# Gate and up stage: the first logit sum of four blocks moved behind the up-weights' sums and parts on VectorE

## The chip, the core and the metric

The kernel runs on one core of one Trainium2 chip. The metric is the device time of one execution in microseconds (us); lower is better.

## What is computed

A token's output is a gated mix of a Fourier layer and a GEGLU layer, with S = 2048 tokens, D = 640, F = 1728, all float32:

```python
g = _sigmoid((x * gate_w).sum(-1, keepdims=True))
a = jnp.einsum("bsd,ed->bse", x, dft_hid_re)
b = jnp.einsum("bsd,ed->bse", x, dft_hid_im)
y = jnp.einsum("ts,bse->bte", dft_seq_re, a) - jnp.einsum("ts,bse->bte", dft_seq_im, b)
b = (_gelu(x @ w_gate) * (x @ w_up)) @ w_down
return g * y + (1 - g) * b
```

The argument of the sigmoid, one number per token, is the *logit* of the title.

## The kernel before

Every matrix product is made of three products of float32r parts (`mm3`, L99 to L103): an operand is split into a high part (ScalarE, `high`, L82) and a low part (VectorE, `low`, L85, what the high part left out), and high x high, low x high and high x low are summed in a bank of 128x512. To save products, blocks of two rows and two columns are multiplied by Strassen's scheme, so VectorE also forms sums and differences of weights, of inputs and of results.

The kernel has four stages: a first block, the gate and up stage (blocks f = 1 to 12 of the 1728 hidden columns), the product with w_down, and the Fourier layer. The change lies in the gate and up stage. Its loop (L1179) issues each block's products from generators (`gate_up`, `together`, `together_up`), and between them takes small pieces of other work from a queue, `fills` (L1153 to L1163): a piece is a cost and a function, and pieces are taken in order, as many as the products issued so far allow. Inside the stage, TensorE, ScalarE, VectorE and POOL keep the order in which the code is written (`in_order`, L107). So the order of `fills` is VectorE's order.

Blocks 5, 7, 9 and 11 are the first of a pair of blocks that share products. In them `fills` holds, ahead of the next block's weights:

- four pieces left over from the block before (`last_sums`, `last_sum`, L578 to L586): differences of results, stored to `hT` by POOL (L404);
- the up-weights across the pair (`make_up`, L241): `across` forms four sums of 128x128 in the raw tile `wu5r` (L246 to L249), `high_u` makes `wu5h` on ScalarE, `low_u` makes `wu5l` (L85); the digit in these names is the block;
- `sum_wd` (L606): sums of down-weights in `dr` and `da` (L595 to L600), stored to `wsd` by SP (L602);
- two logit sums (`load_z`, L709): each loads a tile `xz` of 128x640 (SP, L716) and multiplies it by the gate weights, with a sum along the row (VectorE, L720, followed by a read-back of the accumulator, also L720). The first tile is loaded ahead of the queue, the second where the first sum is done.

Other names in the rows: `pH5t`, `pZ5t` and `pH5u`, `pZ5u` are banks of the shared products, for gate and up; L454 adds `pH5t` to a result that frees the bank, as the copies by ScalarE at L148 do; `xq` and `xu` are shared inputs, loaded anew by POOL in each such block (`load_across`, L1150), three `xu` tiles in each; `hA` and `hT` are stores of results by POOL; L309 forms a difference in the raw weights of the next block, which ScalarE then splits.

Tiles of 4 KB a partition, `xz` among them, share a pool of 46 buffers (`slot`, L72). A tile gets a buffer that an earlier tile gave back, in the order in which the code asks, and the first writer of the new tile waits for the last reader of the old one.

Of the kernel before, what the change touches and what calls it, by code (L numbers as in the profile page):

```python
# [37 lines left out]
def kernel(  # L38
# [68 lines left out]
    @contextmanager  # L107
    def in_order(*engines):

        traced = nc.cur_bb.bb.instructions  # L110
        mark = traced[-1]
        yield
        start = next(k for k in reversed(range(len(traced))) if traced[k] is mark) + 1
        dep = mybir.DependencyInfo(mybir.DependencyClass.NoSync, mybir.DependencyReason.DATA)
        prev = {}
        for ins in traced[start:]:
            if ins.engine in engines:
                if ins.engine in prev:
                    tc.add_manual_dep(ins, prev[ins.engine].name, dep, reason="in_order")
                prev[ins.engine] = ins  # L120
# [84 lines left out]
    def pair_of(f):  # L205


        return 0 if f < PAIRED or f >= NF else 2 - (f - PAIRED + 1) % 2
# [18 lines left out]
    def load_up(f):  # L227

        r = slot(F32, [P, 8, P], f"wu{f}r")
        nc.sync.dma_start(r[:, 0:2], wf[f, :, 2:4])  # L230
        nc.sync.dma_start(r[:, 6:8], wf[f - 1, :, 2:4])
        return r
# [8 lines left out]
    def make_up(f, r):  # L241

        W, own = {}, {}

        def across():
            tt(r[:, 2], r[:, 0], r[:, 1], op=ALU.add)  # L246
            tt(r[:, 4], r[:, 6], r[:, 0], op=ALU.subtract)
            tt(r[:, 3], r[:, 2], r[:, 6], op=ALU.subtract)
            tt(r[:, 5], r[:, 7], r[:, 3], op=ALU.subtract)  # L249

        def high_u():
            own["u"] = [slot(F32R, [P, 8, P], f"wu{f}{n}") for n in "hl"]
            high(own["u"][0][:, 1:6], r[:, 1:6])

        def low_u():
            u = own["u"]
            low(u[0][:, 1:6], u[1][:, 1:6], r[:, 1:6])
            W["A22p"] = at(u, 1)
            for k in range(4):
                W[f"S{k + 1}p"] = at(u, 2 + k)  # L260

        return W, [(112, across), (0, high_u), (78, low_u)]
# [343 lines left out]
    def sum_wd(k):  # L606

        work = []

        def load():  # L610
            r, a21 = slot(F32, [P, 8, P], f"dr{k}"), wsmall(F32, f"da{k}")
            nc.sync.dma_start(r, wd[k, :, :8])
            nc.sync.dma_start(a21, wd[k, :, 8:])
            work.extend(do for _, do in sums_left(nc.sync, r[:, 0:2], r[:, 2:4], r[:, 6:8], a21, wsd[k]))

        def do():
            work.pop(0)()

        return [(0, load), (84, do), (84, do)]
# [89 lines left out]
    def load_z(n):  # L709

        r, work = {}, []

        def load():
            sb = zq.pop(0)
            r[0] = sb, slot(F32, [P, D], f"xz{sb}")
            nc.sync.dma_start(r[0][1], xz[sb])  # L716

        def total():
            sb, v = r.pop(0)
            nc.vector.tensor_tensor_reduce(v, v, gwb, 1.0, 0.0, ALU.mult, ALU.add, z[:, sb : sb + 1])  # L720

        return [(0, load), (80, total)] * n
# [66 lines left out]
    def load_k(i):  # L789


        tp, b, k = kseq[i]
        n = f"{tp}{b}{k}"
        r = None
        if not (k == NK and b):
            r = slot(F32, [P, 8, P], f"kw{n}")
        if k == NK and b:
            src = hL[tp]
        elif k == NK:
            m = slot(F32, [P, 8, P], f"km{n}")  # L800
            d = slot(F32, [P, 8, P], f"kd{n}")
            nc.sync.dma_start(r[:, :5], wd0)
            for q in range(2):
                rows = slice(q * FR, (q + 1) * FR)
                nc.sync.dma_start(m[rows, :5], wdr)
                nc.sync.dma_start(d[rows, :4], wd0[:FR, :4])
            r, src = (r, m, d), h0[tp]
        elif b:
            nc.sync.dma_start(r[:, 0:2], wd[k, :, 6:8])
            nc.sync.dma_start(r[:, 2:8], wsd[k][:, 0:6])  # L810
            src = hT[tp][k]
        else:
            nc.sync.dma_start(r[:, 0:6], wd[k, :, 0:6])
            nc.sync.dma_start(r[:, 6:8], wsd[k][:, 6:8])
            src = hA[tp][k]
        raw = []
        for q in range(2):
            raw.append(pair(F32, f"kr{n}{q}"))
            nc.sync.dma_start(raw[q], src[:, 2 * q : 2 * q + 2])
        kraw[i] = r, raw  # L820
# [332 lines left out]
    fills, state = deque(), {}  # L1153
# [24 lines left out]
    with in_order(PE, ACT, DVE, POOL):  # L1178
        for f in range(1, NF):  # L1179
            kind = pair_of(f)  # L1180
            if f == PAIRED:
                loadu()
                fills.extend([*t4, *u123[:3], *late_work, *u123[3:], *u4])
            fills.extend(todo)
            todo.clear()
            if kind == 1:
                up, work = make_up(f, load_up(f))
                fills.extend(work)
            if kind == 1:
                lw, *w = sum_wd((f - PAIRED) // 2)  # L1190
                lw[1]()
                fills.extend(w)
            if f == PAIRED - 1:
                loadp()
                fills.extend(t123)
            if f == NF - 1:
                lw, *w = sum_wd(NK - 1)
                lw[1]()
                fills.extend(w)
            if f + 1 < NF:  # L1200
                nxt, work = make_w(f + 1)
                if kind != 1 or f == PAIRED:
                    fills.extend(work)
            if kind == 1 and f > PAIRED:
                (_, first), z1, (_, second), z2 = load_z(2)
                first()
                k = len(fills) // 2
                more = list(fills)
                fills.clear()
                fills.extend([*more[:k], z1, (0, second), *more[k:], z2, *work])  # L1210
            elif f in ZE_AT:
                (_, first), z1 = load_z(1)
                first()
                fills.insert(5, z1)
            if f == NF - 1:
                load_k(0)
                fills.extend(split_pieces(0))
                gates(0)
                nc.scalar.activation(table, table, AF.Gelu_apprx_tanh)
            state.update(pe=0, done=0, all=sum(c for c, _ in fills), pe_all=2450 if not kind else 2994 if kind == 1 else 1768)  # L1220
            s5 = pair(F32, f"s5{f}")
            xs = {}
            work = [gate_up(f, W, Bs[tp], tp, s5[:, tp], s1t, xs, s4) for tp in range(2)]
            more = together(f, W, Tp, s1t, xs) if kind == 1 else iter(())
            more_up = together_up(f, W, up, s4) if kind == 1 else iter(())
            store_left()
            if f in LEFT_AT:
                left_work.extend(LEFT_AT[f]())
                if f in (2, 12):
                    k = len(fills) // (2 if f == 2 else 1)  # L1230
                    rest = [fills.pop() for _ in range(len(fills) - k)]
                    fills.extend([*left_work, *reversed(rest)])
                    state["all"] = sum(c for c, _ in fills)
                    left_work.clear()
            for _ in range(4):
                run(more)
            for step in range(8 if not kind else 7):
                for tp, w in enumerate(work):
                    run(w)
                    if (step, tp) in ((0, 1), (1, 1)):  # L1240
                        run(more)
                        if step == 0:
                            run(more)
                    if (2, 0) < (step, tp) < (6, 0):
                        run(more_up)
                if step < 2 and kind == 1 and f > PAIRED:
                    for k in ((1,), (2, 3))[step]:
                        load_across(f, "xu", Tu, keptu, k)
                if step == 4 and pair_of(f + 1) == 1 and f + 1 > PAIRED:
                    for k in (1, 2, 3):  # L1250
                        load_across(f + 1, "xq", Tp, keptp, k)
                if step == 5:
                    load_w(f + 2)
                if f == NF - 1 and step > 4:
                    load_k(step - 4)
            for v in (more, more_up):
                next(v, None)
            while fills:
                fills.popleft()[1]()
            W = nxt  # L1260
# [438 lines left out]
```

## Time and profile before

| what | value |
|---|---|
| median of 3 runs | 1020.55 us (1020.52 to 1021.36) |
| the profiled execution, its own time | 1021.83 us |
| its span, first to last instruction | 1020.0 us |
| TensorE busy (PE), weight loads (PEld) | 1015.6 us, 840.2 us |
| VectorE busy (DVE) | 823.2 us |
| ScalarE busy (ACT) | 486.1 us |
| GpSimd busy (POOL) | 166.9 us |
| granted TensorE clock | 1.00 |

How to read it: busy time is the time in which an engine executes; weight loads run beside the products before. Rows of a timeline give the start, the duration, the engine, the source line, the operation and "out<-in", and in brackets how long the engine sat idle before it and what ended that. "SPq" is a row of a queue that only issues DMAs. An `x2` counts merged rows. Times in the text are from the start of the span. Blocks 5, 7, 9 and 11 lie at about 145, 193, 241 and 289 us.

### The profile page before, as it was taken

Reading aid. Unit: us, or ns where it says so; the run is one execution under the profiler, and the core shown is the slowest. Engines: PE = TensorE matmul, PEld = TensorE weight load, DVE = VectorE, ACT = ScalarE, POOL = GpSimd, SP = SyncE. Lnnn points to the kernel's source line nnn. Section 1 sums busy time; section 2 is a strip of 40 time slices with the busy share of each in tenths; the row PEclk is TensorE's granted clock in tenths of the full one; section 3 lists DMA queues with packets and bytes.
Section 4 is the critical chain, followed back from the end, with each engine's and each line's share of the span. In section 5 each row is a group of like instructions: output and inputs, shape, how many; then the busy total and the mean of one; then the engine's idle time right before and its main releaser. Section 6 shows DMA issues by size and latency. Waiting matters only on the chain.

```text
span 1020.0 us, 13269 instructions
## 1 busy us (share of the span) xinstructions
PE 1015.6 (100%) x4483; PEld 840.2 (82%) x4483; DVE 823.2 (81%) x1154; ACT 486.1 (48%) x622; POOL 166.9 (16%) x295
## 2 busy tenths in 40 slices
PE   9999999999999999999999999999999999999998
PEld 7888888888888888888888888888888888888887
DVE  6987877787787989888887976898588869797796
ACT  5544534353535667557444443444344444455440
POOL 0122242323231200100001012102210200021112
PEclk9999999999999999999999999999999999999999
DMA  7468588968699999979874669668866877897856
GB/s 271 168 209 276 181 264 275 314 225 290 201 315 313 415 374 383 330 245 329 295 254 172 213 223 337 223 200 298 302 203 209 294 252 275 295 349 215 274 134 99
DMA packets 96644, 267.58 MB, mean 262 GB/s; under 512 B 12672, under 2 KB 27008, under 8 KB 96576
## 3 DMA queue, kind: packets, MB, share of 16 engines
q1 hardware_dynamic: 70512, 185.24, 53.2%
q0 software_dynamic: 25776, 81.30, 24.4%
q8 instruction: 35, 0.57, 0.2%
q14 instruction: 33, 0.27, 0.1%
q10 hardware_dynamic: 288, 0.20, 0.1%
HBM read 192.48 MB, written 70.27 MB: 258 GB/s over the span
## 4 chain that ended last, share of the span: by engine, by line
PE 97%; issue 1%; DMA 1%; DVE 0%; POOL 0%; POOLq 0%
PE pX L103 6%; PE pX L102 6%; PE pX L101 6%; PE pZ L103 4%; PE pZ L102 4%; PE pZ L101 4%; PE pL L102 3%; PE pL L103 3%; PE pL L101 3%; PE pV L102 2%; PE pV L103 2%; PE pV L101 2%; PE pY L102 1%; PE pR L103 1%; PE pQ L101 1%; PE pQ L102 1%
## 5 line engine op out<-in xcount | busy, mean ns | idle before, releaser
L82 ACT ACTIVATE ch<-csa 128x1024 fp32r<-128x1024 f32 x32 | 34.0, 1063 | 78.2 <-DVE csa L770 76.7
L85 DVE TENSOR_TENSOR cl<-cra,ch 128x1024 fp32r<-128x1024 f32 x32 | 39.1, 1222 | 24.6 <-ACT ch L82 22.5
L82 ACT ACTIVATE ch<-cra 128x1024 fp32r<-128x1024 f32 x32 | 33.9, 1059 | 52.3 <-DVE cl L85 19.3
L85 DVE TENSOR_TENSOR cl<-crb,ch 128x1024 fp32r<-128x1024 f32 x32 | 39.1, 1223 | 14.4 <-ACT ch L82 14.4
L102 PE MATMUL pL<-cl,xah 128*128 128x512 f32 x128 | 49.9, 390 | 0.0
L103 PE MATMUL pL<-ch,xal 128*128 128x512 f32 x128 | 49.9, 390 | 0.0
L101 PE MATMUL pL<-ch,xah 128*128 128x512 f32 x128 | 49.7, 390 | 0.0
L82 ACT ACTIVATE ch<-crb 128x1024 fp32r<-128x1024 f32 x32 | 33.8, 1055 | 31.2 <-PE pL L102 11.4
L404 POOL DMA_DIRECT2D hA<-s x48 | 26.1, 544 | 132.7 <-DVE s L562 113.1
L85 DVE TENSOR_TENSOR cl<-csb,ch 128x1024 fp32r<-128x1024 f32 x32 | 39.2, 1225 | 3.7 <-ACT ch L82 2.3
L85 DVE TENSOR_TENSOR cl<-csa,ch 128x1024 fp32r<-128x1024 f32 x32 | 39.1, 1221 | 2.1 <-ACT ch L82 1.1
L82 ACT ACTIVATE ch<-csb 128x1024 fp32r<-128x1024 f32 x32 | 34.0, 1062 | 11.7 <-DVE csb L773 4.7
L556 ACT ACTIVATE s<-s 128x512 f32<-128x512 f32 x24 | 15.2, 633 | 46.7 <-DVE s L555 46.7
L148 ACT ACTIVATE s<-pX 128x512 f32<-128x512 f32 x40 | 23.5, 598 | 23.7 <-PE pX L103 22.4
L85 DVE TENSOR_TENSOR kl<-kw,kh 128x1024 fp32r<-128x1024 f32 x24 | 29.4, 1223 | 4.5 <-DMA kw<-in_wd 2.6
L82 ACT ACTIVATE kh<-kw 128x1024 fp32r<-128x1024 f32 x24 | 25.3, 1052 | 16.1 <-PE kR L103 6.2
L551 DVE TENSOR_TENSOR s<-s,pX 128x512 f32<-128x512 f32 x24 | 16.5, 686 | 19.6 <-PE pX L103 14.3
L1346 POOL DMA_DIRECT2D uA<-c x8 | 4.3, 542 | 168.9 <-DVE c L1448 168.7
L404 POOL DMA_DIRECT2D hT<-s x48 | 26.0, 541 | 24.3 <-DVE s L579 8.1
L929 POOL DMA_DIRECT2D out<-ks x12 | 6.5, 541 | 136.8 <-DVE ks L928 136.2
L101 PEld LDWEIGHTS pL<-ch,xah 128*128 128x128 f32 x128 | 24.0, 188 | 5.0
L102 PEld LDWEIGHTS pL<-cl,xah 128*128 128x128 f32 x128 | 24.0, 188 | 5.0
(3612 smaller groups left out, 3483.8 us busy)
## 6 DMA issues: line engine op xcount, KB each, us to landing
cra<-in_ct SPq DMA_DIRECT2D x64, 512.0 KB, 4.6
crb<-in_ct SPq DMA_DIRECT2D x64, 512.0 KB, 5.0
hA<-s POOLq DMA_DIRECT2D x48, 256.0 KB, 5.9
hT<-s POOLq DMA_DIRECT2D x48, 256.0 KB, 5.7
kr<-hA SPq DMA_DIRECT2D x24, 512.0 KB, 7.7
kr<-hT SPq DMA_DIRECT2D x24, 512.0 KB, 6.8
ux<-uA SPq DMA_DIRECT2D x24, 512.0 KB, 5.9
ux<-uT SPq DMA_DIRECT2D x16, 512.0 KB, 6.7
```

The lines of the kernel that those rows point to most:

```text
L82: nc.scalar.activation(hi, raw, AF.Copy)
L85: nc.vector.tensor_tensor(lo, raw, hi.bitcast(F32), op=ALU.subtract)
L101: nc.tensor.matmul(ps, lh, rh, start=first, stop=False, skip_group_check=True)
L102: nc.tensor.matmul(ps, lh, rl, start=False, stop=False, skip_group_check=True)
L103: nc.tensor.matmul(ps, ll, rh, start=False, stop=last, skip_group_check=True)
L148: nc.scalar.activation(m, src, AF.Copy)
L404: nc.gpsimd.dma_start(to[:, i], src)
L551: tt(s5, s5, X, op=ALU.add)
L556: nc.scalar.activation(s2, s2, AF.Gelu_apprx_tanh)
L929: nc.gpsimd.dma_start(acc4[:, t] if tp and e == 4 else out[2 * tp + t, e], src)
L1346: nc.gpsimd.dma_start(to[:, i], src)
```

## The change

One number changes, the place in the queue at which the first sum `z1` and the second load are put:

```diff
             if kind == 1 and f > PAIRED:
                 (_, first), z1, (_, second), z2 = load_z(2)
                 first()
-                k = len(fills) // 2
+                k = len(fills) - 2
                 more = list(fills)
                 fills.clear()
                 fills.extend([*more[:k], z1, (0, second), *more[k:], z2, *work])
```

`fills` has nine pieces there (four left over, three of the up-weights, two of the down-weights), so k goes from 4 to 7: the first sum and the second load stood behind the left-over pieces, and now stand behind the up-weights.

VectorE in block 5 (`xz` and `z` are the logit sum; the number behind a name tells tiles apart):

```order
-L720 ISA xz_1411,z<-xz_1411,gwb 128x640
-L720 ISA z 128x1
-L454 TENSOR_TENSOR s_1431<-s_1431,pH5t 128x512
 L246 TENSOR_TENSOR wu5r<-wu5r 128x128
 L247 TENSOR_TENSOR wu5r<-wu5r 128x128
 L248 TENSOR_TENSOR wu5r<-wu5r 128x128
 L249 TENSOR_TENSOR wu5r<-wu5r 128x128
+L454 TENSOR_TENSOR s_1431<-s_1431,pH5t 128x512
 L459 TENSOR_TENSOR s_1450<-s_1450,pZ5t 128x512
 L460 TENSOR_TENSOR s_1450<-s_1450,pX_1_1461 128x512
 L85 TENSOR_TENSOR wu5l<-wu5r,wu5h 128x640
+L720 ISA xz_1411,z<-xz_1411,gwb 128x640
+L720 ISA z 128x1
 L595 TENSOR_TENSOR dr_1407<-da_1408,dr_1407 128x256
```

The first sum goes from ahead of the up-weights' sums to behind `wu5l`; L454 goes behind the four small sums. Blocks 7, 9 and 11 read the same.

SP in block 5, with the semaphores that each issue waits for (DMAHW and DMASW tell of landed transfers, the others of engines):

```order
 L612 DMA dr1_1407<-in_wd 128x1024 [waits DMASW4_49,DMAHW3_49,DMASW1_49,PE_49]
 L716 DMA xz0_1411<-in_xz 128x640 [waits DMASW4_49,DMASW6_49,DVE_49,DMAHW4_49,PE_49,Activation_49]
-L716 DMA xz1_1482<-in_xz 128x640 [waits DMASW7_49,DMASW5_49,DMAHW5_49,PE_49,Activation_49]
+L716 DMA xz1_1513<-in_xz 128x640 [waits DMAHW2_49,DMAHW5_49,DMAHW1_49,DVE_49]
 L602 DMA wsd1_128<-dr1_1407 128x256 [waits DMAHW6_49,DMAHW3_49,DVE_49]
 L602 DMA wsd1_128<-da1_1408 128x256 [waits DMAHW7_49,DVE_49]
 L602 DMA wsd1_128<-dr1_1407 128x256 [waits DMAHW0_49,DVE_49]
```

The second `xz` load keeps its place in SP's order but has another buffer: it waited for a product on TensorE, and now it waits for VectorE, for L85 `wu5l`, the last reader of `wu5r`, whose buffer it takes. In blocks 7 and 9 it is the same; in block 11 the buffer is one that stores of `hT` read.

POOL in block 5:

```order
 L404 DMA hT11_84<-s53_985 128x512 [waits DMASW1_49,DVE_49]
 L404 DMA hT11_84<-s54_1257 128x512 [waits DMASW2_49,DVE_49]
-L1150 DMA xu51_1490<-xv1_562 128x1024 [waits DMASW3_49,PE_49]
-L1150 DMA xu52_1532<-xv2_563 128x1024 [waits DMAHW1_49,DMAHW2_49,DMASW4_49,DVE_49]
+L1150 DMA xu51_1487<-xv1_562 128x1024 [waits DMASW3_49,PE_49]
+L1150 DMA xu52_1532<-xv2_563 128x1024 [waits DMASW4_49,DVE_49]
 L1150 DMA xu53_1534<-xv3_564 128x1024 [waits DMASW5_49,PE_49]
```

The order is kept, but the second `xu` load (`xu52`) had the buffer of `wu5r` and waited for L85 `wu5l`; now it has the buffer of the first `xz` tile and waits for the first logit sum. Blocks 7 and 9 read the same; in block 11 it waits for a store of `hT`, before and now.

## The prediction, made before the changed kernel ran

> **What bounds the kernel now.** I read the page first, then the waits of TensorE's weight loads in the stretch that holds the four blocks, then the timelines of one of them, engine by engine.
>
> ```profile
> PE 1015.6 (100%) x4483; PEld 840.2 (82%) x4483; DVE 823.2 (81%) x1154; ACT 486.1 (48%) x622; POOL 166.9 (16%) x295
> ```
>
> TensorE is busy for 1015.6 of 1020.0 us, so 4.4 us are idle in the whole span. The list of waits for 150 to 320 us (who waited, for whom, us in total, times, longest) shows what of this lies in the stage:
>
> ```profile
> PEld pH7u L101 <- DMA xu<-xv: 0.5, 1, 0.5
> PEld pH7t L101 <- DVE s L454: 0.2, 1, 0.2
> ```
>
> Two waits, both in block 7. What the first costs shows in the matmul starts (start, duration, engine, line):
>
> ```profile
> 212.27 0.39 PE L102 MATMUL pX<-xT03l,ws7h 128*128 128x512 f32 x1
> 212.50 0.39 PE L103 MATMUL pX<-xT03h,ws7l 128*128 128x512 f32 x1
> 213.01 0.50 PE L101 MATMUL pH7u<-xu,wu7h 128*128 128x512 f32 x1
> 213.34 0.40 PE L102 MATMUL pH7u<-xu,wu7h 128*128 128x512 f32 x1
> ```
>
> Matmuls start 0.23 apart; here 0.51 and 0.33, so 0.28 + 0.10 = 0.38 us are lost. The stage can therefore **give at most 0.38 + 0.2 = 0.6 us** to any reordering, less than 0.2% of the time (2.04 us), about what a measurement of this kernel can tell from no change. What is left to ask is whether the change makes TensorE wait, and for how long.
>
> **The change part by part.** No instruction is added or taken away; four times, one sum of 128x640 moves on VectorE, and one load moves in time. Block 5 on VectorE:
>
> ```profile
> 150.19 0.69 DVE L585 TENSOR_TENSOR s<-s,s 128x512 f32<-128x512 f32 x1
> 153.50 0.83 DVE L720 CUSTOM_DVE_ANT_0 xz<-xz,gwb 128x640 f32<-128x640 f32 x1 [2.62 <-DMA hA<-s]
> 154.25 0.08 DVE L720 DVE_READ_ACCUMULATOR2_ANT z<- 128x1 f32 x1
> 154.25 0.68 DVE L454 TENSOR_TENSOR s<-s,pH5t 128x512 f32<-128x512 f32 x1
> 154.85 0.28 DVE L246 TENSOR_TENSOR wu5r<-wu5r 128x128 f32<-128x128 f32 x1
> ...
> 155.78 0.68 DVE L459 TENSOR_TENSOR s<-s,pZ5t 128x512 f32<-128x512 f32 x1
> ...
> 158.22 0.82 DVE L85 TENSOR_TENSOR wu5l<-wu5r,wu5h 128x640 fp32r<-128x640 f32 x1 [1.04 <-DMA hT<-s]
> 158.97 0.42 DVE L595 TENSOR_TENSOR dr<-da,dr 128x256 f32<-128x256 f32 x1
> ```
>
> *What gets earlier.* The first sum stalls VectorE for 2.62 us at its old place. Without it the four sums of L246 to L249 follow L585 directly (0.60 behind 150.19, as L246 is 0.60 behind L454) and take 0.93 (154.85 to 155.78), so L454 starts at 150.19 + 0.60 + 0.93 = 151.7 instead of 154.25. That is 2.5 us of margin, but only block 7 waits for L454: a gain of 0 to 0.2 us. I take nothing, since a weight load runs ahead of its matmul. The rest of the gain ends at L85 wu5l: it waited 1.04 us for a store of hT, and still does.
>
> *What gets later: the second xu load.* In the changed program it takes the buffer of the first sum's tile, so it waits for that sum, where it waited for L85 wu5l:
>
> ```profile
> 159.45 1.13 POOL L1150 DMA_DIRECT2D xu<-xv  x2 [4.31 <-DVE dr L595]
> xu<-xv POOLq DMA_DIRECT2D x1, 512.0 KB, 5.2
> 164.78 0.19 PEld L101 LDWEIGHTS pH5u<-xu,wu5h 128*128 128x128 f32 x1
> ```
>
> Now L85 wu5l ends at 158.22 + 0.82 = 159.04, and the issue follows 0.41 later. Then the sum starts at 158.97 (where L595 stands) and its read-back ends 0.75 + 0.08 later, at 159.80: **0.76 us later**. The load (the second row is the DMA view of 159.3 to 159.7: KB, us to landing) lands at 159.45 + 5.2 = 164.65 now, and the weight load that needs it starts at 164.78: 0.13 spare. So block 5 would lose 0.76 - 0.13 = 0.63 us, and block 7, whose weight load waits already, all 0.76. In block 9:
>
> ```profile
> L1150 POOL DMA_DIRECT2D xu<-xv x2: 537/544/551, 254.5 to 255.1; - x2
> L101 PEld LDWEIGHTS pH9u<-xu,wu9h x1: 188/188/188, 260.6 to 260.6; 128*128 128x128 f32 x1
> ```
>
> With 5.2 to land it is there at 259.7, 0.9 early, which covers 0.76: nothing. In block 11 the load takes the buffer of a tile that a store of hT reads, not that of the sum; issued at 302.0 and needed at 308.3, it has 1.1 spare, and I count nothing there either:
>
> ```profile
> L1150 POOL DMA_DIRECT2D xu<-xv x2: 540/544/548, 302.0 to 302.6; - x2
> L101 PEld LDWEIGHTS pH11u<-xu,wu11h x1: 188/188/188, 308.3 to 308.3; 128*128 128x128 f32 x1
> ```
>
> The Trainium skill's page "DMA: Bandwidth & Descriptors", section "Anatomy of one DMA — SWDGE (gpsimd) path", fits a load that POOL issues as 2.0 us plus its bytes over 436 GB/s, which for 512 KB gives an estimate of 3.2 us; by that the load would be there 2 us before its use and this whole term would be 0. The row says 5.2, with other transfers around it, and the measurement decides.
>
> *What takes some of it back: the second xz load leaves a crowded place.* The pair of loads in block 5 (first and last start, then us to landing):
>
> ```profile
> L716 SPq DMA_DIRECT2D xz<-in_xz x2: 327/328/328, 144.8 to 147.5; - x2
> ...
> DMA to landing us min/median/max: 7.8/8.2/8.5
> ```
>
> The second was issued at 147.5, in the burst at a block's start, and needed 7.8 us; now it goes into the buffer of wu5r and waits for L85 wu5l, the last reader. First the engines' windows (the last columns are the clock, the DMA share and GB/s), then the two queues from 151.8 to 154.3 us:
>
> ```profile
> 148.00:152.00 4.00, 4.00 (x19) 3.31 (x18) 2.88 (x5) 0.04 (x1) 1.73 (x4) 1.00 1.00 396
> 152.00:156.00 4.00, 4.00 (x19) 3.33 (x18) 2.47 (x8) 0.05 (x1) 1.63 (x3) 1.00 1.04 419
> 160.00:164.00 4.00, 4.00 (x19) 3.27 (x18) 3.72 (x10) 3.97 (x9) 0.54 (x2) 1.00 0.84 206
> ...
> q0 software_dynamic: 225, 0.73, 71.8%
> q1 hardware_dynamic: 144, 0.31, 31.6%
> ```
>
> From 148 to 156 the DMA engines are full (share 1.00 and 1.04), and the 0.31 MB on the hardware queue are about the size of one xz tile (320 KB). At 419 GB/s it takes 0.78 us of them, so the stores of hT behind it, and with them L85 wu5l, come 0 to 0.78 us earlier. The middle is nearest to what the rows say: the store waits for room until 152.4 (POOL's row "152.44 0.54 ... <-DMA hA<-s" stands before most of that traffic), and only its own way from there gains. I take 0.4. In the other direction, the late load now lies beside the xu loads. From 160 to 164 only 206 of 419 GB/s move, but the share is 0.84, so 0 to 0.4 us (half of 0.78) on xu; I take 0.1.
>
> ```profile
> 152.44 0.54 POOL L404 DMA_DIRECT2D hT<-s  x1 [0.49 <-DMA hA<-s]
> ```
>
> **The sum.** Block 5: 0.76 - 0.4 + 0.1 - 0.13 = 0.33. Block 7: 0.76 - 0.4 + 0.1 = 0.46. Blocks 9 and 11: 0. Together **+0.8 us**. The profiled execution took 1021.83 us (span 1020.0, the rest around it), so its like would take 1022.6; the median of the runs is 1020.55, 1.28 lower, and there the sum gives **1021.3 us**, within 0.2%.
>
> **The rivals.**
>
> *The second sum waits for its own load (slower).* This is the dangerous part of the edit: the load is issued about 11 us later, and behind the second sum VectorE holds the next weights' differences, for which ScalarE waits, in order, before it copies the bank that TensorE needs back.
>
> ```profile
> L716 SPq DMA_DIRECT2D xz<-in_xz x1: 328/328/328, 167.9 to 167.9; - x1
> xz<-in_xz SPq DMA_DIRECT2D x1, 320.0 KB, 3.1
> 160.68 0.82 DVE L720 CUSTOM_DVE_ANT_0 xz<-xz,gwb 128x640 f32<-128x640 f32 x1
> 165.88 0.60 ACT L148 ACTIVATE s<-pH5u 128x512 f32<-128x512 f32 x1 [1.34 <-PE pH5u L103]
> 166.82 0.19 PEld L101 LDWEIGHTS pH5u<-xu,wu5h 128*128 128x128 f32 x1
> wsd<-da SPq DMA_DIRECT2D x1, 128.0 KB, 5.0
> ```
>
> In the burst such a load needs about 8, in a quiet place (issued at 167.9) 3.1. The new place is quiet on SP's queue, since the four wsd stores stand behind it in program order, so I take 3.1. Issued at the end of L85 wu5l, 159.04 less the 0.4 won, it lands at 161.7. Pushed by the first sum alone, the second would start at 160.68 + 0.75 - 0.4 = 161.0, so VectorE waits 0.7 us. TensorE does not notice: ScalarE has 1.34 idle before the copy, and the copy ends at 166.48, 0.34 before the weight load, so the second sum may start as late as 160.68 + 1.68 = 162.36. With the 0.33 that TensorE itself is then late, the load may take 162.7 - 158.6 = **4.1 us; from there each us costs a us in each block**. At 5.0, as a wsd store in just this place needs, it is 0.9 in two to four blocks; with three, 2.7 + 0.8 = 3.5, or 1024.1 us. For it speaks the xu loads nearby; against it, that the load is issued ahead of the xu load and the stores.
>
> *The relief is whole (the same, a little lower).* If the hT stores gain all of 0.78, the first sum's delay is gone: block 5 and 7 lose nothing, 1020.5 us. For it speaks that the DMA engines are full at that place, so that each KB taken out should count; against it, that POOL issues those stores only as older ones land. The Trainium skill's page "DMA: Bandwidth & Descriptors", section "Issuing engines are not separate DMA queues", says that DMAs of all issuing engines run on the same 16 DMA engines and interleave; by that, this rival is the outcome. The two queue rows above, which share the engines 71.8 to 31.6, agree.
>
> *Faster.* If in addition the xu load of block 7 came early and L454's wait went, at most 0.6 us are won, 1020.0 us, still within 0.2%. Only something that no row shows could give more.
>
> **How the numbers follow.** The forecast, 1021.3, has 0.5; its own range, with relief from 0.78 to 0 and xu 0 to 0.4 slower, is 1020.5 to 1020.55 + (1.03 + 1.16) = 1022.7. The late load that holds VectorE back has 0.25, whole relief 0.2, a gain beyond that 0.05. The range for all reaches from 1020.1 to 1024.2: it leaves out the upper half of the first rival and a little below. Slower by over 0.2% means above 1022.6: nearly all of the first rival and a sliver of the forecast, 0.24. Faster by over 0.2% means below 1018.5: 0.02. The rest, 0.74, is within 0.2%.
>
> **What would show it.** In block 5 after the change: L454 near 151.7 and no idle 2.62 ahead of it; the first sum near 158.6, directly behind L85 wu5l, whose idle time before it is then longer; the second xu issue 0.3 to 0.8 after 159.45; the second xz load issued at the end of L85 wu5l and landing in 3 to 4 us; under 1 us of idle VectorE before the second sum; ScalarE's copy of pH5u still waiting for TensorE, not for VectorE. In the list of TensorE's waits, pH5u and pH7u behind xu stand with some tenths, and no pH line behind ScalarE. I am wrong if that landing takes over 4.1 us: then pH5u and its like wait for L148 in several blocks. I am also wrong if a wait turns up after 330 us, since the buffers of later tiles are handed out in another order too.

## The result and the profile after

| what | before | after |
|---|---|---|
| median | 1021.29 us (15 runs, 1020.52 to 1022.94) | 1023.64 us (15 runs, 1021.88 to 1026.21) |
| ratio to before | | 1.0026, 95% interval 1.0019 to 1.0033 |
| the profiled execution | 1021.83 us, span 1020.0 | 1026.11 us, span 1024.3 |

By the ratio the change makes the kernel slower by 0.26%; the medians lie 2.35 us apart (predicted: 0.8). The profiled execution of after is one of its slowest; a second one, below, took 1022.87 us, so the first shows the effect enlarged. Each group of experiments below has runs of before on its own chip beside it: e1 to e4 18 runs with a median of 1021.33 us, the kernels with g 33 runs and 1021.23, those with h 21 runs and 1021.53.

The waits of TensorE's weight loads from 150 to 320 us, after, first in that execution and then in the second one (g0):

```profile
PEld pH9u L101 <- DMA xu<-xv: 2.2, 1, 2.2
PEld pH7u L101 <- DMA xu<-xv: 1.4, 1, 1.4
```

```profile
PEld pH7u L101 <- DMA xu<-xv: 1.6, 1, 1.6
PEld pH9u L101 <- DMA xu<-xv: 0.7, 1, 0.7
```

Block 7 waited 0.5 us before, and block 9 did not wait. The wait for L454 is gone. VectorE in block 5, after:

```profile
151.52 0.68 DVE L454 TENSOR_TENSOR s<-s,pH5t 128x512 f32<-128x512 f32 x1
...
157.11 0.82 DVE L85 TENSOR_TENSOR wu5l<-wu5r,wu5h 128x640 fp32r<-128x640 f32 x1 [3.59 <-DMA hT<-s]
157.86 0.82 DVE L720 CUSTOM_DVE_ANT_0 xz<-xz,gwb 128x640 f32<-128x640 f32 x1
...
158.60 0.42 DVE L595 TENSOR_TENSOR dr<-da,dr 128x256 f32<-128x256 f32 x1
...
160.76 0.82 DVE L720 CUSTOM_DVE_ANT_0 xz<-xz,gwb 128x640 f32<-128x640 f32 x1 [0.36 <-DMA xz<-in_xz]
```

All moves as foreseen: L454 2.7 us earlier, the first sum directly behind L85 `wu5l`, and L85 itself 1.1 us earlier (157.11, was 158.22), since the store of hT for which it waits lands earlier. So the second xu load is issued earlier in block 5, not later. Its rows in blocks 5, 7 and 9 (the first load of each row is the second xu load; the last column of a landing row is the third's):

```profile
159.09 1.14 POOL L1150 DMA_DIRECT2D xu<-xv  x2 [4.81 <-DVE dr L595]
```

```profile
L1150 POOL DMA_DIRECT2D xu<-xv x2: 547/548/548, 206.7 to 207.3; - x2
...
DMA to landing us min/median/max: 6.8/7.3/7.8
```

```profile
255.30 1.13 POOL L1150 DMA_DIRECT2D xu<-xv  x2 [4.44 <-DVE dr L595]
```

Issued at 159.09 (was 159.45), 206.7 (was 207.7) and 255.30 (was 254.48, with TensorE 0.6 us behind its place in before by then). The time to landing is what grew: 6.8 us in block 7 (5.3 before), and in block 9 the DMA view has

```profile
xu<-xv POOLq DMA_DIRECT2D x1, 512.0 KB, 8.0
wsd<-dr SPq DMA_DIRECT2D x1, 128.0 KB, 5.1
wsd<-da SPq DMA_DIRECT2D x1, 128.0 KB, 7.8
```

where before had 5.2 for xu in the same place (the smallest of these three is the second load's):

```profile
DMA to landing us min/median/max: 5.2/5.7/6.2
```

255.30 + 8.0 = 263.3 is when TensorE goes on; its matmuls there:

```profile
261.18 0.39 PE L103 MATMUL pX<-xT03h,ws9l 128*128 128x512 f32 x1
263.35 0.50 PE L101 MATMUL pH9u<-xu,wu9h 128*128 128x512 f32 x1 [1.79 <-DMA xu<-xv]
263.69 0.39 PE L102 MATMUL pH9u<-xu,wu9h 128*128 128x512 f32 x1
...
264.61 0.62 PE L103 MATMUL pX<-xT13h,ws9l 128*128 128x512 f32 x1
265.03 0.63 PE L101 MATMUL pX<-xT13h,ws9h 128*128 128x512 f32 x1
265.46 0.63 PE L102 MATMUL pX<-xT13l,ws9h 128*128 128x512 f32 x1
```

The starts are 2.17 apart, 1.94 more than the usual 0.23, and the next pair 0.34, 0.11 more. Then, from 264.61 to 268.02, eight matmuls start 0.43 apart instead of 0.23: the granted clock fell (0.70 from 265 to 270), and 8 x 0.20 = 1.6 us more are lost. In block 7 the same two gaps are 1.34 and 0.34:

```profile
212.25 0.39 PE L103 MATMUL pX<-xT03h,ws7l 128*128 128x512 f32 x1
213.59 0.50 PE L101 MATMUL pH7u<-xu,wu7h 128*128 128x512 f32 x1 [0.95 <-DMA xu<-xv]
```

Sum: block 7 1.11 + 0.11, block 9 1.94 + 0.11 + 1.6, together 4.9; less the 0.38 that block 7 lost before, and the 0.2 for L454, 4.3 us. The profiled executions differ by 1026.11 - 1021.83 = 4.28, so these two blocks account for it.

What fills that time is seen in the windows from the issue of the second xu load in block 9 to its landing, before and then after (the last two columns are the DMA share and GB/s). Within them lie the xu load of POOL and, in after, the late xz load of SP:

```profile
254.40:259.70 5.30, 5.30 (x25) 4.34 (x24) 4.37 (x12) 4.82 (x11) 1.09 (x2) 1.00 0.77 209
```

```profile
255.20:263.30 8.10, 6.37 (x28) 4.88 (x26) 5.12 (x13) 5.24 (x10) 1.08 (x2) 1.00 0.85 241
```

1.11 MB went through before and 1.95 MB after, at 209 and 241 GB/s. At such rates, not at the 419 of the burst, the moved tile of 0.33 MB costs 1.4 to 1.6 us. But 0.84 MB more went through, not 0.33. The two queues (POOL's, then SP's; packets, MB, share) show where, before and then after:

```profile
q0 software_dynamic: 219, 0.82, 61.6%
q1 hardware_dynamic: 315, 0.29, 15.8%
```

```profile
q0 software_dynamic: 283, 1.02, 47.0%
q1 hardware_dynamic: 700, 0.92, 36.9%
```

SP's queue moved 0.63 MB more, of which the tile is at most 0.33, and POOL's 0.20 more. The rest is other traffic: more of the wsd stores, of the next weights' load and of the third xu load goes through before the second xu load has landed. Whether that is cause or consequence of the longer flight, the rows don't tell.

### The profile page after: what moved, and what is told of

Same layout as the page of the kernel before. It is cut to its first block, busy times and chain, and to the rows that moved or that the text cites. A ratio compares the mean times of both kernels' runs of the same rounds, so it can differ in the third digit from the quotient of the medians.

```text
span 1024.3 us, 13265 instructions
## 1 busy us (share of the span) xinstructions
PE 1017.0 (99%) x4483; PEld 840.4 (82%) x4483; DVE 823.2 (80%) x1154; ACT 486.9 (48%) x622; POOL 166.9 (16%) x295
## 4 chain that ended last, share of the span: by engine, by line
PE 94%; DMA 2%; issue 2%; DVE 1%; POOL 1%; SPq 0%; ACT 0%; POOLq 0%
PE pX L103 6%; PE pX L102 6%; PE pX L101 6%; PE pZ L101 4%; PE pZ L102 4%; PE pZ L103 4%; PE pL L101 3%; PE pL L102 3%; PE pL L103 3%; PE pV L101 2%; PE pV L102 2%; PE pV L103 2%; DMA xu<-xv 1%; PE pY L101 1%; PE pR L101 1%
## 5 line engine op out<-in xcount | busy, mean ns | idle before, releaser
L85 DVE TENSOR_TENSOR cl<-cra,ch 128x1024 fp32r<-128x1024 f32 x32 | 39.1, 1223 | 24.6 <-ACT ch L82 22.4
L85 DVE TENSOR_TENSOR cl<-crb,ch 128x1024 fp32r<-128x1024 f32 x32 | 39.1, 1222 | 14.9 <-ACT ch L82 14.8
L85 DVE TENSOR_TENSOR cl<-csb,ch 128x1024 fp32r<-128x1024 f32 x32 | 39.2, 1225 | 3.7 <-ACT ch L82 2.3
L85 DVE TENSOR_TENSOR cl<-csa,ch 128x1024 fp32r<-128x1024 f32 x32 | 39.1, 1221 | 2.1 <-ACT ch L82 1.1
L148 ACT ACTIVATE s<-pX 128x512 f32<-128x512 f32 x40 | 23.7, 596 | 24.6 <-PE pX L103 24.1
L537 ACT ACTIVATE s<-pZ 128x512 f32<-128x512 f32 x24 | 13.9, 595 | 39.5 <-PE pZ L103 22.0
L85 DVE TENSOR_TENSOR kl<-kw,kh 128x1024 fp32r<-128x1024 f32 x24 | 29.2, 1218 | 3.8 <-DMA kw<-in_wd 2.6
L103 PEld LDWEIGHTS pL<-ch,xal 128*128 128x128 f32 x128 | 24.0, 188 | 5.0
```

The source lines that it names most:

```text
L85: nc.vector.tensor_tensor(lo, raw, hi.bitcast(F32), op=ALU.subtract)
L103: nc.tensor.matmul(ps, ll, rh, start=False, stop=last, skip_group_check=True)
L148: nc.scalar.activation(m, src, AF.Copy)
L537: nc.scalar.activation(s5, Z, AF.Copy)
```

## The experiments

Two theories of the loss stood at first. **Theory 1**: the late xz load shares the DMA engines with the second xu load and stretches it. **Theory 2**: the xu load is issued later, since it waits for the first sum. A third came up on the way: it is mostly the four wsd stores that stretch the xu load. In the diffs, `more[:4]` are the four left-over pieces, `more[4:7]` the up-weights, `more[7:]` the down-weights with their stores, and k is 7.

### The late sum alone: e1_load_early

```diff
-                fills.extend([*more[:k], z1, (0, second), *more[k:], z2, *work])
+                fills.extend([*more[:4], (0, second), *more[4:k], z1, *more[k:], z2, *work])
```

(Here, in e3 and in e4, `load_z` also keeps its loaded tiles in a list, so that two can be loaded ahead.)

> The first sum stands where the change puts it, but the second xz load is issued early, in the burst, as before; the second xu load still waits for the first sum. Theory 1, the late load's traffic slows the xu load and that is what TensorE waits for: the xu loads land 5.2 us after issue as before, and only the 0.76 us by which they are issued later is left, at most 0.6 to 1.4 us over before. Theory 2, the time went into the later issue of the xu load: as the changed kernel, 2 to 3 us over before, with xu landings of 5.2 us and waits of 0.7 us or more in blocks 5, 7 and 9.

Measured: 1024.77 us (8 runs), ratio 1.0032 (1.0022 to 1.0043). Weight loads wait for xu in all three blocks:

```profile
PEld pH7u L101 <- DMA xu<-xv: 1.5, 1, 1.5
PEld pH5u L101 <- DMA xu<-xv: 1.3, 1, 1.3
PEld pH9u L101 <- DMA xu<-xv: 1.2, 1, 1.2
```

Two more wait for ScalarE's L474, 0.3 and 0.2 us. The load itself needs 5.2 to 5.4 us, as before; it is issued 0.8 to 1.8 us later than before, relative to its use. So theory 2's cost is real where nothing gives it back. It is more than the 0.76 of one sum: with the xz load early, L85 also came 0.1 to 1.1 us later than before. In blocks 5 and 7 it waited for ScalarE's `wu5h` and `wu7h`, so this kernel isn't a clean half of the change.

### The late load alone: e2_load_late

```diff
+                fills.extend([*more[:4], z1, *more[4:k], (0, second), *more[k:], z2, *work])
```

> The first sum stands where it was, and only the second xz load is late, behind the up-weights; the second xu load waits for L85 wu5l as before. Theory 1, the late load's traffic: xu landings of 6.5 to 8 us in blocks 7 and 9, waits of TensorE of 1 to 2 us there, 1 to 3 us over before. Theory 2, the later issue: the xu load is issued as early as before or 0.4 to 0.8 earlier, so within 0.5 us of before or a little below.

Measured: 1023.34 us (11 runs), ratio 1.0017 (1.0008 to 1.0026).

```profile
PEld pH9u L101 <- DMA xu<-xv: 1.3, 1, 1.3
PEld pH7u L101 <- ACT s L148: 1.2, 1, 1.2
```

With the first sum at its old place, the xu load is issued earlier than in before in all three blocks, relative to its use, and yet needs 5.3, 6.0 and 8.1 us, and block 9 waits. That is theory 1, with block 7 a little below its 6.5 to 8. Block 7's wait is the prediction's first rival: there the second xz load lands only after 5.8 us, and VectorE stands before the second sum:

```profile
DVE xz L720 <- DMA xz<-in_xz: 4.6, 1, 4.6
```

### The late load behind the xu load: e3_load_after

```diff
+                fills.extend([*more[:k], z1, *more[k:], (0, second), *work[:5], z2, *work[5:]])
```

> The first sum is late as in the change, the second xz load stands behind the down-weights' stores and its sum behind the next block's low parts; the second xu load waits for L85 again. Theory 1: the xz load is now behind the second xu load and the stores on the engines, so the second xu load lands in 5 to 6 us and the time is within 1 us of before. Theory 2: the same, since the first sum holds no xu load any more. If the xu load still needs 7 us or more, neither order of issue nor the load's place counts but its bytes in this stretch.

Measured: 1041.37 us (4 runs), ratio 1.0190 (1.0172 to 1.0208). Both theories missed. The xu load indeed landed in 4.2 to 4.5 us, but TensorE waits for ScalarE's L474:

```profile
PEld pV5u L101 <- ACT pV5u L474: 5.7, 1, 5.7
PEld pV9u L101 <- ACT pV9u L474: 4.3, 1, 4.3
PEld pV7u L101 <- ACT pV7u L474: 3.8, 1, 3.8
```

The row on ScalarE ahead of it names the cause in block 5:

```profile
166.96 0.63 ACT L82 ACTIVATE wa<-wa6r 128x512 fp32r<-128x512 f32 x1 [6.27 <-DMA wsd<-dr]
```

The high part `wa` is written into a buffer that a wsd store reads. That store lands no later than usual: the last of block 5 at 166.88, against 166.57 in before, where `wa` was written at 162.42 without a wait. So `wa` now has another buffer than in before. A reordering that draws a tile from the shared pool at another point hands out later buffers anew (read from the code, not from a row); this kernel measures that more than it measures the load.

### Both sums at the end: e4_sums_end

```diff
+                fills.extend([*more[:4], (0, second), *more[4:], z1, z2, *work])
```

> Both sums stand behind the down-weights' sums, both loads are early; the second xu load waits for the first sum, which is now 0.75 + 4 x 0.46 = 2.6 us later than L85's end was. Theory 2's price by itself: block 5 loses 2.5 us, block 7 2.6, block 9 1.7, block 11 nothing or a little, together 6 to 7 us over before, and more if the clock drops in a wait that long. If later issue costs nothing, the time is within 0.5 us of before.

Measured: 1025.26 us (5 runs), ratio 1.0038 (1.0025 to 1.0050). The xu load is issued 2.5 to 3.6 us later than in before, relative to its use, but TensorE waits for it for only 1.1 to 1.4 us in each block, because it lands sooner. Waits for ScalarE's L537 (0.8 us in two) and L474 (0.5 us in blocks 5 and 7) come on top. The rows of block 5, the landing of the second and third xu load and the wsd stores:

```profile
L1150 POOL DMA_DIRECT2D xu<-xv x2: 540/546/551, 162.2 to 162.8; - x2
...
DMA to landing us min/median/max: 3.4/3.9/4.3
```

```profile
wsd<-dr SPq DMA_DIRECT2D x3, 128.0 KB, 1.8
wsd<-da SPq DMA_DIRECT2D x1, 128.0 KB, 1.8
```

Here two of the four wsd stores have landed before the second xu load is issued, and the last lands 0.7 us after that: 3.4 us for xu instead of 5.2, and 1.8 for a store instead of the 5 to 6 of the last three. Both theories had taken 5.2 for granted. This is what suggested the third theory, and the next four runs.

### The changed kernel again: g0_after_again

> The changed kernel, unaltered, for another profiled execution. Theory 1 (the late xz load shares the DMA engines with the second xu load) expects that load again to need more than 5.8 us in at least two of the blocks 5, 7 and 9, and a wait of TensorE for it of 0.5 to 2.5 us in each of those; a clock drop behind a wait of about 2 us. Theory 2 (the later issue) expects some 5.2 us to landing and equal waits of 0.5 to 0.8 us in blocks 5 and 7. Time about 1023.6.

Measured: 1023.39 us (11 runs), ratio 1.0023 (1.0014 to 1.0031); the profiled execution took 1022.87. Its waits stand above, beside those of after. To landing the xu load needs 5.5, 6.3 and 7.0 us in blocks 5, 7 and 9, so it is long in blocks 7 and 9 in both executions, while in block 5 it lands 0.4 to 0.7 us ahead of its use in both. The clock doesn't fall here, where the longest wait is 1.6 us.

### The late load made tiny: g2_late_tiny

```diff
-            nc.sync.dma_start(r[0][1], xz[sb])
+            nc.sync.dma_start(*((r[0][1][:, :16], xz[sb][:, :16]) if sb in (1, 4, 7, 9) else (r[0][1], xz[sb])))
...
-            nc.vector.tensor_tensor_reduce(v, v, gwb, 1.0, 0.0, ALU.mult, ALU.add, z[:, sb : sb + 1])
+            nc.vector.tensor_tensor_reduce(v, gwb if sb in (1, 4, 7, 9) else v, gwb, 1.0, 0.0, ALU.mult, ALU.add, z[:, sb : sb + 1])
```

> The changed kernel, with the second xz load of each of the four blocks cut to 16 of 640 columns (8 KB instead of 320 KB), in the same place, buffer and order; the second sum multiplies the gate weights by themselves in its place, so that VectorE is as busy (the logit of these four tiles is left out). Theory 1 expects the xu load back at 4.5 to 5.4 us in blocks 7 and 9, no wait of over 0.4 us and 1020.3 to 1021.5. Theory 2 expects the waits and the time of the changed kernel, 1.1 to 2.2 us and 1023.6, since the issue is as late as there. Theory 3 expects 5.2 us to landing and 1021 too, so it differs from theory 1 only in the first kernel of wsd stores.

Measured: 1021.26 us (11 runs), ratio 1.0000 (0.9991 to 1.0009). No weight load waits from 140 to 330 us. Order, buffers, waits and VectorE's work are those of the changed kernel; only 312 of 320 KB are gone, and the second sum reads the gate weights in place of the tile. The xu load is issued 5.9 to 6.4 us ahead of its use (5.5 to 5.9 in after, 4.8 to 6.4 in g0; 5.3, 4.8 and 6.1 in before), and needs:

```profile
L1150 POOL DMA_DIRECT2D xu<-xv x2: 540/544/548, 253.2 to 253.8; - x2
...
DMA to landing us min/median/max: 5.2/5.7/6.2
```

5.2 us in block 9 where after had 8.0, and 5.3 in block 7 where it had 6.8. With after's issue, 5.9 us ahead, 5.2 us would still have been in time. **This settles what the loss needs: it comes with the bytes of the late load, and without them the place of the issue costs nothing.** Theory 2 falls as the cause of the loss. It isn't quite absent from single executions: in block 7 of g0 the load was issued 4.75 us ahead of its use, so that even a landing after 5.3 us would have left some 0.5 of the 1.6 us.

### Half and three quarters of it: g3_late_half, h2_late_480

The same edit with `:320` and `:480` for `:16`.

> As the one before, but 320 of 640 columns are loaded (160 KB); the second sum again multiplies the gate weights by themselves. Theory 1 expects a point between: the xu load at 5.2 to 6.8 us in blocks 7 and 9, waits of 0.3 to 1.2 us there, 1021.5 to 1023. Theory 2 expects the changed kernel's waits and 1023.6.

Measured: 1021.33 us (11 runs), ratio 1.0001 (0.9992 to 1.0009), no waits, and 5.4 and 5.5 us for xu in blocks 7 and 9: theory 1's interval for the xu load held at its lower end, those for the waits and the time were missed.

> The changed kernel, with 480 of 640 columns of each late xz tile loaded (240 KB), the second sum again over the gate weights by themselves (the logit of these tiles is left out). With 160 KB the second xu load needed 5.4 and 5.5 us in blocks 7 and 9, with 320 KB 6.3 to 8.0. If the contention grows evenly with the bytes: 5.8 to 6.8 us, waits of 0 to 0.9 us, about 1022. If it starts where the load no longer lies between two other transfers: either 5.5 us and 1021.3, or as in the changed kernel, 1023.5.

Measured: 1021.63 us (11 runs), ratio 1.0004 (0.9995 to 1.0013); 5.7 and 5.5 us in blocks 7 and 9, 7.2 in block 11.

```profile
PEld pH7u L101 <- DMA xu<-xv: 1.1, 1, 1.1
PEld pH11u L101 <- DMA xu<-xv: 0.8, 1, 0.8
```

The wait in block 7 goes more with the issue, 4.7 us ahead of the use as in g0, where after, g2 and g3 have 5.5 to 5.9. So the price doesn't grow evenly with the bytes: up to 240 KB the xu load needs 5.0 to 5.7 us in blocks 5, 7 and 9, and with 320 KB 4.8 to 8.0. Why it jumps so, and in which block, isn't shown by these runs. The smaller loads also have shorter rows (1920 and 1280 bytes instead of 2560), and no run separates that from the bytes.

### The wsd stores out of the way: g1_wsd_behind, h1_wsd_last

g1 is the order of before with the down-weights behind the second sum; h1 is that of after with the same.

```diff
+                fills.extend([*more[:4], z1, (0, second), *more[4:k], z2, *more[k:], *work])
```

```diff
+                fills.extend([*more[:k], z1, (0, second), z2, *more[k:], *work])
```

> The kernel before, with the down-weights' sums and their four wsd stores put behind the second logit sum; both xz loads stay early. Theory 3 (it is mostly the wsd stores that stretch the xu load) expects it to land in 3.4 to 4.3 us instead of 5.2, and the one wait of before, 0.5 us in block 7, to be gone: 1020.3 to 1021.0. Theory 1 alone expects 5.2 us as in before and no change of time, 1021.3, as no load has come in beside it.

Measured: 1020.96 us (11 runs), ratio 0.9998 (0.9989 to 1.0007). The xu load lands in 4.2 to 4.5 us instead of 5.2, at and a little above the upper end of what theory 3 expected; the stores are now issued from 0.7 us behind it on, where the first went out with it. No weight load waits for the xu load any more; two others wait 0.5 us each. In block 5:

```profile
L1150 POOL DMA_DIRECT2D xu<-xv x2: 540/544/548, 158.9 to 159.6; - x2
...
DMA to landing us min/median/max: 4.4/5.0/5.6
```

The time hardly answers: the prediction's bound of 0.6 us for any reordering of this stage is seen here from the other side.

> The changed kernel, with the down-weights' sums and their four wsd stores put behind the second logit sum. If it takes both the late xz load and the wsd stores to slow the second xu load (theory 1 with theory 3), it lands in 4 to 5.3 us and TensorE does not wait for it. In exchange VectorE waits some 2 us for the late load and has the next weights' differences 1.8 us later; ScalarE had 1.0 us idle before its copy of pH5u and the copy 0.34 to spare, so by the prediction's first rival TensorE waits 0.4 to 0.6 us for L148 in two to four blocks: 1022 to 1023.5. If the late load alone slows it, it needs over 6 us and the time is 1024 or more.

Measured: 1022.32 us (11 runs) beside 1021.53, ratio 1.0011 (1.0002 to 1.0020). With the whole late load, but with the wsd stores issued only 3.0 to 3.7 us behind it, the xu load needs 4.1, 4.5 and 4.9 us, and nobody waits for it. Block 9, where after had 8.0:

```profile
L1150 POOL DMA_DIRECT2D xu<-xv x2: 538/543/548, 254.0 to 254.6; - x2
...
DMA to landing us min/median/max: 4.9/5.3/5.7
```

It takes the late load **and** the stores to make it late. In exchange the first rival of the prediction turns up:

```profile
PEld pH7u L101 <- ACT s L148: 0.9, 1, 0.9
PEld pH9u L101 <- ACT s L148: 0.2, 1, 0.2
```

VectorE waits for the late load and does the down-weights after it, and ScalarE's split comes late (block 5):

```profile
160.09 0.83 DVE L720 CUSTOM_DVE_ANT_0 xz<-xz,gwb 128x640 f32<-128x640 f32 x1 [2.24 <-DMA xz<-in_xz]
```

In block 5 the copies behind it had just enough margin; in blocks 7 and 9 they had not.

## Why the prediction came out as it did

The time, 1023.64 us, lies inside the range of 1020.1 to 1024.2, but above the forecast's own range (1020.5 to 1022.7), and the ratio, 1.0026, falls in the case that got a chance of 0.24. That it lies inside is luck: the upper part of the range was drawn for the first rival, which was not at work, and the loss is three times the forecast one. Of the 2.3 us by which the time misses the forecast of 1021.3, 0.7 are the base, whose first three runs had a median of 1020.55 where all 15 have 1021.29. Step by step:

- **What bounds the kernel, and the bound of 0.6 us on any gain**: right. TensorE is the limit before and after, and g1, which removes every wait for xu, is at 0.9998.
- **L454 earlier, 0 to 0.2 us gained, taken as nothing**: right; 151.52 where 151.7 was worked out, and its wait of 0.2 us in block 7 is gone.
- **The second xu load issued 0.76 us later**: right as a mechanism (its issue now follows the first sum, directly), but outweighed. g2, where the same order costs nothing, prices it at zero net of the relief. Block 5, forecast to lose 0.33 us, lost nothing.
- **The relief of 0.4 us**: too small. Taken relative to TensorE's need for xu, L85 `wu5l` starts 0.9, 1.5 and 0.5 us earlier in blocks 5, 7 and 9, so that the xu load is issued 0.15 and 0.7 us earlier in blocks 5 and 7 and 0.24 later in block 9. With the sum late and the load left in the burst (e1), L85 starts 0.1 to 1.1 us later than in before, so the earlier start does come with the moved load. The second rival's mechanism, whole relief, took place; its time did not follow.
- **The step that failed: the contention on xu, "0 to 0.4 us (half of 0.78) on xu; I take 0.1".** Measured: +1.5 us in block 7 and +2.8 in block 9 in the profiled execution, +1.0 and +1.8 in g0, and -0.3 and +0.3 in block 5. The bytes were divided by 419 GB/s, the rate of the burst that the load leaves. The place it goes to moves 206 GB/s at a share of 0.84, by the very row that was quoted beside the estimate; 0.33 MB at 206 are 1.6 us, and that should have been the upper bound at least. A share of 0.84 at half the rate (against 1.04 at 419 GB/s) says that this place is nearly as busy as the burst, not half empty. Even 1.6 is less than block 9's 2.8, in whose flight 0.84 MB more were moved; why it is so much there is open.
- **Block 9 counted at nothing because of 0.9 us to spare**: wrong for the same reason; the spare was weighed against the delay of the issue alone.
- **The second sum waiting for its load (first rival, 1024.1)**: its time was near, its mechanism was not at work. The late xz load landed in 2.8 to 3.7 us, VectorE waited 0.36 us in block 5, 1.3 in block 9 and 3.8 in block 11 (under 1 was expected), and ScalarE's copy of `pH5u` still had 1.00 us idle, ended by TensorE. No weight load waits for L148 in after. In e2 (landing after 5.8 us) and h1 it does, for 1.2 and up to 0.9 us, so the mechanism is real. That landings of up to 3.7 us cost nothing in after, and one of 5.8 us a wait in block 7 of e2, fits the break-even of 4.1, but it isn't tested: in block 11 of e2 a landing after 5.8 us cost nothing either, and in block 7 of h1, with the stores' sums behind the second sum, 3.5 us were too long.
- **Not foreseen: the clock.** In the profiled execution 1.6 of the 4.3 us are matmuls that start 0.43 instead of 0.23 us apart, behind a gap of 2.17. In g0 they are absent. A part of the spread of after (1021.88 to 1026.21, against 1020.52 to 1022.94 before) may come from this; that was not measured.

The Trainium skill's page "DMA: Bandwidth & Descriptors", section "Issuing engines are not separate DMA queues", on which the prediction leant for the relief, says that transfers of all issuing engines interleave on the same 16 DMA engines. The trace agrees, but at both ends of the move: a load that SP issues slowed one that POOL issues from 5.2 to 8.0 us. A rule that prices what a transfer gives back where it leaves also prices what it costs where it arrives, and the prediction used it for the first alone.

## What to carry to other kernels

A transfer that is moved takes its cost along: price it at the rate that the new place moves (here 0.33 MB at 206 GB/s, an estimate of 1.6 us), not at the rate of the place that it leaves, and look up which waited-for transfer is in flight there. Take that as a rough size and no bound: the xu load took from 0.3 us less to 2.8 us more in blocks 5, 7 and 9 with 320 KB beside it, and 0.3 to 0.4 more with 240 KB. Spare time of a consumer has to cover a longer landing as well as a later issue. To tell "issued later" from "lands later", shrink the suspected transfer to a few bytes and leave its order, buffer and waits alone.

## What the runs showed of the hardware

- One load of 512 KB that POOL issues landed in 3.4 to 3.6 us with SP's four wsd stores issued well ahead of it (e4), in 4.1 to 4.9 with the stores issued from 0.7 us or more behind it on (g1, e3, h1), in 5.2 to 5.3 with the first store issued together with it (before), and in 4.8 to 8.0 beside those and a load of 320 KB (after, g0). A wsd store of 128 KB took 1.8 to 1.9 us ahead of the xu load (e4) and 4.5 to 8.7 beside it and the late load (after). All of this is from blocks 5, 7 and 9.
- The load of 320 KB, 7.8 us in the burst at a block's start, took 2.8 to 3.7 us at its new place, beside the very transfers that it slowed: it was issued 1.1 us ahead of the xu load. In block 7 of e2, where only 0.04 us lay between the two, it took 5.8 us.
- A gap of 2.17 us in the matmul starts was followed, from 1.3 us after the restart, by eight matmuls 0.43 us apart instead of 0.23; gaps of up to 1.55 us in other executions were not. The length alone doesn't decide it: in e3, gaps of 5.69 and 4.24 us were followed by such a stretch, and one of 3.80 us (start of `pV7u` at 221.09) was not. The Trainium skill's page "TensorE: Matmul & The Clock Gate", section "What's actually happening", puts the idle window behind which the clock is halved at about 3.4 us, free-running. The 3.40 us of idle TensorE ahead of e3's row at 221.09, without a slow stretch, agree with that; the 1.79 us in after, with one, do not, and here less was enough.
